# Moving a partition-group exchange from one load per group into four stores per pair, with one product stage a step later

## The chip, the core and the metric

The kernel runs on one NeuronCore of a Trainium2 chip, in one launch. The metric is device time in microseconds (us). Before the change, three runs took 1902.69, 1904.52 and 1907.6 us, so the median is 1904.52 us. Inputs and outputs are float32; each operand of a matmul is split into a high and a low part (float32r), and three products of the parts stand for one.

## The reference, cut to what matters

The input `x` has 2048 rows of 512. After a layer norm it goes through an attention with 32 heads over the last 512 cached keys and values, and through a gated branch, and the two are multiplied:

```python
xn = _layernorm(x)
# A: 32 heads, Dh = 128, keys and values cut to the last W = 512
q = (xn @ wq).reshape(B, Sq, Hq, Dh).transpose(0, 2, 1, 3)
scores = einsum("bhqd,bhkd->bhqk", q, k) * (Dh ** -0.5)
p = softmax(scores)
o = einsum("bhqk,bhkd->bhqd", p, v)
s = o.transpose(0, 2, 1, 3).reshape(B, Sq, Hq * Dh) @ wo
# B: z = gelu(xn @ w_in), halves z1 and layernorm(z2); w_sp mixes the rows
g = silu(((w_sp @ z2) + b_sp) * z1 @ w_out)
return x + s * g
```

The change concerns only how `p` is turned around between the softmax and the product with `v`, and when `q` is computed.

## The kernel before

The attention is cut into 128 blocks: one head and 512 query rows each (`NBLK = H * NQ`). A block has four steps of 128 query rows, and a counter `t` runs over all 512 steps, with a lead before and a tail after. The work is written as a software pipeline by hand: at each `t`, the loop at L680 to L730 issues one piece of each stage, and each stage works on a different block. The order in which a step's pieces are written is the order on each engine. For block b, whose first step is t = 4b:

- `score` (L468, steps 4b to 4b+3): three matmuls give a 128x512 tile of scores in PSUM, VectorE takes the negated maximum (L475), ScalarE the exponential with its row sums (L477). Rows of the tile are queries, columns are keys.
- `turn` (L479, one step later): the product with `v` needs keys on the partitions. VectorE transposes 32x32 squares (L486) into the tile `pB`, which holds two steps. This leaves four groups of 32 partitions that have yet to be exchanged among each other. The exchange goes through DRAM: after every second step one store (L491) writes `pB`, 128 rows of 4 KB, to `p_dram`.
- `turned` (L495, at t = 4b+7): four loads (L499) read the block back. Load a fills the 32 partitions 32a to 32a+31 of `pL`, with 8 pieces of 1 KB for each partition. These loads make the exchange.
- `shares` (L501, steps 4b+11 to 4b+14): ScalarE makes the high part `pT_h` (L506), GpSimd the low part `pT_l` (through the helper at L59).
- `pv` (L510, steps 4b+13 to 4b+16): three matmuls a step into a PSUM tile `ps_a`; `pv_out` (L515) at the last one makes `oT_h` and `oT_l`.
- `outp` (L526, steps 4b+18 to 4b+21): the product with `wo`, added to `sacc` by VectorE (L536).

`q` is computed in groups of four blocks (two heads, two query halves) in seven products instead of eight, `q_products` (L439), 42 matmuls spread over 16 steps, in three PSUM tiles `ps_a` of which one is held for the whole group. The group g starts at step 16g - `LEAD`, and everything that belongs to it is placed relative to that step: its weight loads (`load_q`, L405), the sums and splits of the weights on GpSimd and ScalarE, the evictions and the final `qT_h` and `qT_l` (`q_out`, L374; its VectorE part is put into the list `late` and issued at L728, at the end of the step). `ps_a` has four buffers (L83), shared by q's three tiles and by the tile of `pv`. The next tile to be allocated takes a buffer that is free, and its first matmul waits for the last reader of what stood there.

The other loads of this phase are pieces of 256 KB of weights, keys and values (`raw`, L102, and `wq`, L409), two a block, and, more rarely, parts of `x`. Every one of these transfers is issued by SyncE (SP), in program order. An issue that must wait for a semaphore holds up all issues behind it. After the attention follow the gated branch's products (L795 to L810) and the mixing of rows with the output (L951 to L977), which the change does not touch.

Of the kernel before, what the change touches and what calls it, by code (L numbers as in the profile page):

```python
# [8 lines left out]
F32 = mybir.dt.float32  # L9
# [8 lines left out]
P = 128  # L18
# [14 lines left out]

XL, QL, ML, PL, OL = 11, 7, 11, 13, 18
T8 = NT // 2
LEAD = 13
Q = 32


# [1 line left out]
def mixer_kernel(ctx: ExitStack, tc: tile.TileContext, x, wh, w_in, w_sp, b_sp, w_out, out):  # L41
# [8 lines left out]
    nc = tc.nc  # L50
# [3 lines left out]
    dram = ctx.enter_context(tc.tile_pool(name="dram", bufs=1, space=DRAM))  # L54
# [309 lines left out]
    pB = [None]  # L364
    qps, qT, pps, pD, pL, pT, oT, prob, sums = {}, {}, {}, {}, {}, {}, {}, {}, {}
# [23 lines left out]
    def qproj(b, c):  # L389
        h, qb = where(b)  # L390
        if c == 0:
            qps[b] = ps_acc.tile([P, 512], F32, name="ps_a")
        mm3(qps[b], c == 0, c == NC - 1, cols(wt[("q", h), 0], c * P, (c + 1) * P),
            tuple(X[0][c // 2, qb][:, a, c % 2] for a in range(2)))
# [84 lines left out]
    def turn(t):  # L479

        b, j = divmod(t, 4)
        if j % 2 == 0:
            pB[0] = ap.tile([P, 4, 2, P], F32, name="pB", bufs=3)
        nc.vector.transpose(pB[0][:, :, j % 2, :].rearrange("p a (c q) -> p a c q", q=Q),  # L486
                            prob.pop(t).rearrange("p (a c q) -> p a c q", a=4, q=Q))
        if j == 0:
            pD[b] = dram.tile([2, P, 1024], F32, name="p_dram", bufs=3)
        if j % 2:  # L490
            nc.sync.dma_start(pD[b][j // 2], pB[0].rearrange("p a j f -> p (a j f)"))  # L491
        if j == 3:
            nc.vector.reciprocal(sums[b], sums[b])

    def turned(b):  # L495
        pL[b] = ap.tile([P, 8, 256], F32, name="pL")
        of = pD.pop(b).rearrange("s (i r) (a f) -> a r (s i) f", i=4, a=4)
        for a in range(4):
            nc.sync.dma_start(pL[b][Q * a:Q * a + Q], of[a])  # L499

    def shares(b, c):  # L501
        hi = ap.tile([P, 512], F32R, name="pT_h", bufs=4)
# [68 lines left out]
    for g in range(1, NG):  # L571
        t0 = 16 * g - LEAD
        loads.setdefault(max(T0, t0 - 12), []).append(g)
# [20 lines left out]
    for k, d in enumerate((4, 6, 8, 11, 13, 15, 17)):  # L594
        for n in range(4):
            ends.setdefault(16 * (NG // 2 - 1) - LEAD + d + (0, 0, 1, 1)[n], []).append((fetch_part, 1, ORDER[k], n))
    ends.setdefault(16 * (NG - 1) - LEAD + 9, []).append((fetch_x, 1, (0, 1)))
    for k in ((0, 0), (1, 0)):
# [81 lines left out]
    for t in range(T0, T1):  # L680
# [9 lines left out]
        i = t + XL  # L690
# [12 lines left out]
        if 0 <= bq < 4:  # L703
            qproj(bq, cq)
        g, s = divmod(t + LEAD, 16)
        if 0 < g < NG:
# [15 lines left out]
        if 0 <= t - 1 < NSTEP:  # L722
            turn(t - 1)
        if t % 4 == 3 and 0 <= t // 4 - 1 < NBLK:
            turned(t // 4 - 1)
# [284 lines left out]
```

## Time and profile before

| what | value |
|---|---|
| three runs, median | 1904.52 us |
| the profiled execution, its own time | 1907.01 us |
| its span, from first to last instruction | 1905.1 us |
| granted TensorE clock, mean | 0.991 |
| steps of the attention, first store of p to last load | 55.4 to 1514.8 us |
| TensorE matmul busy in the span | 96% |
| mean busy share of the 16 DMA engines, 50 to 1510 us | 0.91 |

The page of the profile gives the busy time of each engine: PE is TensorE's matmuls, PEld its weight loads, DVE is VectorE, ACT ScalarE, POOL GpSimd, SP SyncE with the issues of transfers. A tile is named without its number; `pL<-p_dram` reads "into pL from p_dram". In a list of waits, "A <- B: 42.3, 30, 7.8" says that A's engine sat idle for 42.3 us in total, 30 times and at most 7.8 us at once, until B was done. In a table by stretches of time, the last columns are the granted clock, the mean busy share of the 16 DMA engines, and the GB/s that they moved. A share slightly over 1 comes from packets being counted whole in the stretch in which they begin.

### The profile page before, as it was taken

To read this page: it belongs to the slowest core of one execution; us is meant where nothing else is said; L and a number is where in the kernel's file an instruction comes from. 1 tells how busy PE (TensorE), PEld (TensorE's weight loads), DVE (VectorE), ACT (ScalarE), POOL (GpSimd) and SP (SyncE) were. 2 spreads that over 40 slices of the span, in tenths; PEclk is the share of its full clock that TensorE was granted. 3 is DMA by queue.
4 is the path that set the end of the run, shared out by engine and by line. 5 is a ranking of instruction groups with operands and counts; after the bars stand their busy time and mean duration, and the time that the engine had idled before them with its cause. 6 is when DMAs were issued, how large, how long until landed. Compare 5 with 4: busy or idle time off the path is not lost.

```text
span 1905.1 us, 28198 instructions
## 1 busy us (share of the span) xinstructions
PE 1820.5 (96%) x8658; PEld 1540.4 (81%) x8658; DVE 1403.3 (74%) x2497; ACT 1179.1 (62%) x2631; POOL 1244.3 (65%) x1185
## 2 busy tenths in 40 slices
PE   8898999999999898999999999999999999999999
PEld 7776777777787686778887877878777899999998
DVE  5687888888888787788888888888888556333433
ACT  4666677777677575667677777777677545333422
POOL 3686798798798786788878888888888435000000
PEclk9998999999999999999999999999999999999999
DMA  5798999999999889999889899988999833545543
GB/s 180 198 282 228 237 264 242 251 265 239 252 264 244 216 248 296 267 270 247 236 239 241 241 241 245 245 237 245 236 246 260 257 134 119 194 146 168 158 134 96
DMA packets 277624, 429.16 MB, mean 225 GB/s; under 512 B 22272, under 2 KB 183808, under 8 KB 276320
## 3 DMA queue, kind: packets, MB, share of 16 engines
q1 hardware_dynamic: 272864, 421.72, 79.4%
q10 hardware_dynamic: 4608, 5.64, 0.8%
q8 instruction: 68, 1.11, 0.3%
q14 instruction: 84, 0.69, 0.1%
HBM read 260.55 MB, written 166.72 MB: 224 GB/s over the span
## 4 chain that ended last, share of the span: by engine, by line
PE 73%; DMA 11%; DVE 7%; ACT 3%; POOL 3%; issue 2%; SPq 1%; ACTq 0%; POOLq 0%; DVEq 0%
PE ps_a L448 11%; PE ps L65 9%; PE ps L67 9%; PE ps L66 9%; PE ps_a L65 7%; PE ps_a L66 6%; PE ps_a L67 6%; DMA pL<-p_dram 4%; PE ps_g L66 4%; PE ps_g L67 4%; PE ps_g L65 4%; DMA p_dram<-pB 2%; DVE sacc L536 2%; DVE pB L486 1%; ACT prob L477 1%
## 5 line engine op out<-in xcount | busy, mean ns | idle before, releaser
L59 POOL TENSOR_TENSOR pT_l<-pL,pT_h 128x512 fp32r<-128x512 f32 x507 | 657.9, 1298 | 265.5 <-ACT pT_h L506 250.7
L477 ACT ACTIVATE prob<-ps,nm 128x512 f32<-128x512 f32 x512 | 352.8, 689 | 290.9 <-DVE nm L475 285.1
L536 DVE SCALAR_TENSOR_TENSOR sacc<-ps,sums,sacc 128x512 f32<-128x512 f32 x496 | 369.6, 746 | 149.2 <-PE ps L67 144.2
L506 ACT CAST pT_h<-pL 128x512 fp32r<-128x512 f32 x512 | 318.1, 621 | 130.8 <-DMA pL<-p_dram 68.3
L448 PE MATMUL ps_a<-x,x 128*128 128x512 f32 x1302 | 378.6, 391 | 7.9 <-ACT qs L455 6.9
L486 DVE STREAM_TRANSPOSE pB<-prob 128x512 f32<-128x512 f32 x512 | 359.0, 701 | 23.2 <-ACT prob L477 22.4
L475 DVE TENSOR_REDUCE nm<-ps 128x1 f32<-128x512 f32 x512 | 338.8, 662 | 8.6 <-PE ps L67 8.5
L448 PEld LDWEIGHTS ps_a<-x,x 128*128 128x128 f32 x1302 | 245.9, 189 | 61.9 <-ACT qs L455 8.3
L59 POOL TENSOR_TENSOR wl<-raw,wh 128x512 fp32r<-128x512 f32 x192 | 249.2, 1298 | 9.0 <-ACT wh L141 9.0
L65 PE MATMUL ps_a<-pT_h,wh 128*128 128x512 f32 x512 | 204.2, 399 | 46.7 <-DVE qT_l L728 42.3
L65 PE MATMUL ps<-wh,qT_h 128*128 128x512 f32 x512 | 204.0, 399 | 8.6 <-DVE sacc L536 5.1
L66 PE MATMUL ps_a<-pT_l,wh 128*128 128x512 f32 x512 | 203.0, 396 | 7.3 <-POOL pT_l L59 7.1
L67 PE MATMUL ps_a<-pT_h,wl 128*128 128x512 f32 x512 | 200.9, 392 | 0.0
L66 PE MATMUL ps<-wl,qT_h 128*128 128x512 f32 x512 | 200.9, 392 | 0.0
L65 PE MATMUL ps<-wh,oT_h 128*128 128x512 f32 x512 | 200.7, 392 | 0.0
L66 PE MATMUL ps<-wl,oT_h 128*128 128x512 f32 x512 | 200.6, 392 | 0.0
L67 PE MATMUL ps<-wh,oT_l 128*128 128x512 f32 x512 | 200.6, 392 | 0.0
L67 PE MATMUL ps<-wh,qT_l 128*128 128x512 f32 x512 | 200.6, 392 | 0.0
L66 PE MATMUL ps_g<-z_l,x 128*128 128x344 f32 x512 | 162.1, 317 | 1.3 <-POOL z_l L59 1.3
L65 PE MATMUL ps_g<-z_h,x 128*128 128x344 f32 x512 | 162.1, 317 | 0.0
L67 PE MATMUL ps_g<-z_h,x 128*128 128x344 f32 x512 | 161.9, 316 | 0.0
L65 PEld LDWEIGHTS ps_a<-pT_h,wh 128*128 128x128 f32 x512 | 96.7, 189 | 79.2 <-DVE qT_l L728 55.0
(203 smaller groups left out, 3235.3 us busy)
## 6 DMA issues: line engine op xcount, KB each, us to landing
p_dram<-pB SPq DMA_DIRECT2D x256, 512.0 KB, 5.2
pL<-p_dram SPq DMA_DIRECT2D x512, 256.0 KB, 5.8
raw<-wh SPq DMA_DIRECT2D x194, 256.0 KB, 6.7
wq<-wh SPq DMA_DIRECT2D x62, 256.0 KB, 6.1
x<-w_sp SPq DMA_DIRECT2D x60, 256.0 KB, 6.0
x_dram<-rawx SPq DMA_DIRECT2D x32, 256.0 KB, 5.6
x<-x_dram SPq DMA_DIRECT2D x28, 256.0 KB, 7.6
u_dram<-uB SPq DMA_DIRECT2D x15, 384.0 KB, 2.3
```

What stands on the lines that cost most here:

```text
L59: engine.tensor_tensor(lo, whole, hi.bitcast(F32), op=OP.subtract)
L65: nc.tensor.matmul(ps, lh, rh, start=first, stop=False)
L66: nc.tensor.matmul(ps, lh, rl, start=False, stop=False)
L67: nc.tensor.matmul(ps, ll, rh, start=False, stop=last)
L448: nc.tensor.matmul(qps[g, bank], wt["q", g, k][a][:, c * P:(c + 1) * P], X[g * 2 // H][ORDER[k]][:, b, c], start=first, stop=r == 5, skip_ ...
L475: nc.vector.tensor_reduce(nm, ps, axis=AX.X, op=OP.max, negate=True)
L477: nc.scalar.activation(prob[t], ps, AF.Exp, bias=nm, accum_out=sums[b][:, j:j + 1])
L486: nc.vector.transpose(pB[0][:, :, j % 2, :].rearrange("p a (c q) -> p a c q", q=Q), prob.pop(t).rearrange("p (a c q) -> p a c q", a=4, q=Q))
L506: nc.scalar.copy(h, p)
L536: nc.vector.scalar_tensor_tensor(at, ps, rs, at, op0=OP.mult, op1=OP.add)
```

## The change

The store of a pair becomes four stores. Store a takes columns 256a to 256a+255 of the pair's 1024 from all 128 partitions of `pB`, as 128 rows of 1 KB, and puts them where the group a of the exchanged tile belongs. `p_dram` of a block is now laid out as four groups a, 32 rows r, two pairs s, four pieces i and 256 elements. The load is a single one of 128 rows of 8 KB. In addition `LEAD` goes from 13 to 12, so every piece of q's work is issued one step later.

```diff
-LEAD = 13
+LEAD = 12
...
         if j == 0:
-            pD[b] = dram.tile([2, P, 1024], F32, name="p_dram", bufs=3)
+            pD[b] = dram.tile([4, Q, 2, 4, 256], F32, name="p_dram", bufs=3)
         if j % 2:
-            nc.sync.dma_start(pD[b][j // 2], pB[0].rearrange("p a j f -> p (a j f)"))
+            for a in range(4):
+                nc.sync.dma_start(pD[b][a, :, j // 2].rearrange("r i f -> i r f"),
+                                  pB[0].rearrange("p a j f -> p a (j f)")[:, a])
...
     def turned(b):
         pL[b] = ap.tile([P, 8, 256], F32, name="pL")
-        of = pD.pop(b).rearrange("s (i r) (a f) -> a r (s i) f", i=4, a=4)
-        for a in range(4):
-            nc.sync.dma_start(pL[b][Q * a:Q * a + Q], of[a])
+        nc.sync.dma_start(pL[b].rearrange("p k f -> p (k f)"), pD.pop(b).rearrange("a r s i f -> (a r) (s i f)"))
```

On the issuing engine SP, in the attention, this is a run of rows before the change. A row gives the line, the transfer and the sizes of the side that is written, outermost first; "x4" stands for four of the same in a row.

```order
L491 DMA p_dram<-pB 128x1024
L499 DMA pL<-p_dram 32x8x256 x4
L102 DMA raw<-wh 128x512
L491 DMA p_dram<-pB 128x1024 x2
L499 DMA pL<-p_dram 32x8x256 x4
L491 DMA p_dram<-pB 128x1024
L102 DMA raw<-wh 128x512 x2
```

The same run after it:

```order
L492 DMA p_dram<-pB 4x32x256 x4
L499 DMA pL<-p_dram 128x2048
L102 DMA raw<-wh 128x512
L492 DMA p_dram<-pB 4x32x256 x8
L499 DMA pL<-p_dram 128x2048
L492 DMA p_dram<-pB 4x32x256 x4
L102 DMA raw<-wh 128x512 x2
```

The places of stores and loads among the other issues stay, the counts change from two stores and four loads a block to eight stores and one load, and the side of a store in DRAM is now written as 4 times 32 rows of 256 elements, where the side in SBUF still has 128 rows.

On TensorE, at the second and third step of a group of q (where q's second tile `ps_a` begins, L448, next to the first matmul of a block's `pv`, L65), this stood before; the brackets name the engines whose semaphores a matmul waits for:

```order
L448 MATMUL ps_a<-x_180,x_737 128x512
L448 MATMUL ps_a<-x_181,x_737 128x512
L65 MATMUL ps_a<-pT_h,wh_6562 128x512 [waits DVE_49]
L66 MATMUL ps_a<-pT_l,wh_6562 128x512 [waits Pool_49]
L67 MATMUL ps_a<-pT_h,wl_6563 128x512
```

and this stands there now:

```order
L448 MATMUL ps_a<-x_180,x_757 128x512
L448 MATMUL ps_a<-x_181,x_757 128x512 [waits DVE_49,Activation_49]
L65 MATMUL ps_a<-pT_h,wh_8396 128x512
L66 MATMUL ps_a<-pT_l,wh_8396 128x512 [waits Pool_49]
L67 MATMUL ps_a<-pT_h,wl_8397 128x512
```

The `pv` matmul that took its buffer over from a `qT_l` of the step just before no longer has a wait for VectorE there; 30 such waits stood in the program, and none stands now. In its place q's second tile waits for an `oT_l` and an `oT_h` (ScalarE) that were issued more than a step earlier.

## The prediction

> **What bounds the kernel now.** I read the page first, for the busy engine, and the DMA part of it.
>
> ```profile
> span 1905.1 us, 28198 instructions
> PE 1820.5 (96%) x8658; PEld 1540.4 (81%) x8658; DVE 1403.3 (74%) x2497; ACT 1179.1 (62%) x2631; POOL 1244.3 (65%) x1185
> DMA packets 277624, 429.16 MB, mean 225 GB/s; under 512 B 22272, under 2 KB 183808, under 8 KB 276320
> p_dram<-pB SPq DMA_DIRECT2D x256, 512.0 KB, 5.2
> pL<-p_dram SPq DMA_DIRECT2D x512, 256.0 KB, 5.8
> wq<-wh SPq DMA_DIRECT2D x62, 256.0 KB, 6.1
> ...
> bsp<-b_sp SPq DMA_DIRECT2D x1, 8.0 KB, 9.3
> ```
>
> TensorE is busy for 96% of the span. The issue rows, of which three and the last stand here, count 1384 transfers in the DMA view. 16 times 1384 is 22144, and with the 128 rows of 64 B of `bsp` that makes the 22272 packets under 512 B. So each transfer of this kernel ended with 16 completion packets, one for each DMA engine: every one was dealt out to all 16.
>
> Next the stretch of the attention as a whole, in the table by stretches: PE busy, PEld, DVE, ACT, POOL, then clock, DMA share and GB/s.
>
> ```profile
> 50.00:1510.00 1460.00, 1387.58 (x6023) 1125.39 (x6022) 1201.98 (x2138) 1006.98 (x2346) 1178.65 (x1109) 0.99 0.91 248
> ```
>
> 1460 us for 128 blocks are 11.41 us a block. TensorE works 1387.58 / 128 = 10.84 us of it, and only 72.4 us are idle in the whole stretch. The DMA engines are busy for 0.91 of it: they are the second bound, close behind. The waits show what ends the idle time:
>
> ```profile
> ACT pT_h L506 <- DMA pL<-p_dram: 68.3, 26, 8.0
> PE ps_a L65 <- DVE qT_l L728: 42.3, 30, 7.8
> ```
>
> The block's load comes late 26 times, and 30 times the first `pv` matmul waits for the buffer that `qT_l` still reads.
>
> **What the transfers cost now.** Short stretches in which one kind of transfer flows give rates: the first microseconds and the later ones of a set of four loads, then keys and weights in rows of 2 KB, then stores of 4 KB rows.
>
> ```profile
> 1009.00:1009.50 0.50, 0.50 (x4) 0.41 (x3) 0.00 (x0) 0.50 (x3) 0.50 (x2) 1.00 0.94 311
> 1009.50:1012.50 3.00, 2.91 (x14) 2.10 (x12) 2.13 (x5) 2.34 (x7) 3.00 (x3) 1.00 1.06 215
> 1014.75:1016.25 1.50, 1.50 (x9) 1.22 (x8) 1.50 (x4) 0.73 (x2) 1.50 (x3) 1.00 0.89 337
> 1004.75:1006.75 2.00, 2.00 (x11) 1.65 (x10) 1.64 (x3) 0.91 (x2) 0.21 (x1) 1.00 0.94 371
> 1026.00:1027.50 1.50, 1.50 (x8) 1.27 (x7) 1.50 (x3) 1.50 (x4) 1.50 (x2) 1.00 0.88 355
> ```
>
> With the issues of SP beside them one sees which transfer is which (start, length, count):
>
> ```profile
> 1007.49 1.80 SPq L499 DMA_DIRECT2D pL<-p_dram  x4
> 1009.39 0.40 SPq L491 DMA_DIRECT2D p_dram<-pB  x1
> 1009.83 1.39 SPq L102 DMA_DIRECT2D raw<-wh  x2
> ```
>
> Divided by 16 engines: the loads' pieces of 1 KB begin at 311 / 16 = 19.4 GB/s an engine, 52.7 ns each, and fall to 215 / 16 = 13.4, 76.2 ns each. Rows of 2 KB go at 337 / 16 = 21.1, and stores of 4 KB rows at 371 / 16 = 23.2 GB/s. So the loads into 32 partitions run at 58% of the stores' rate. Speeding these up is what the change can gain.
>
> **The change part by part.**
>
> *The single load.* 1 MB a block in 128 rows of 8 KB, 8 rows and 65,536 B for each engine: at the stores' 23.2 GB/s 2.83 us, against 65,536 / 13.4 = 4.88 now. That is 2.05 us less of each engine's time a block, if it is dealt out to 16. Both its sides are written as 128 rows, like those of most transfers so far, and I take that.
>
> *The four stores.* Eight transfers a block, each of 128 pieces of 1 KB. Here the rows of the order matter: the DRAM side is now 4x32x256, the SBUF side still 128 rows. For work to be dealt out by rows, both sides have to be cut into the same number of shares along their outermost size. 128 and 128, or 32 and 32, can be cut in 16; 4 and 128 only in 4. No transfer of the trace has an outermost size that isn't a multiple of 16, so the trace does not show what happens; the bounds are 16 engines and 4. I take 4: an issue carries no more than the sizes and steps of both sides, and 4 is the largest count that both outermost sizes can be cut into. Then 12 of the 16 engines get none of these stores, and I take it that the same four get all of them: 8 x 128 / 4 = 256 pieces of 1 KB a block on each of the four.
>
> [...]
>
> *What a piece costs on such an engine.* The trace has no store in 1 KB pieces. Nearest are the first half microsecond of the 1 KB loads, 52.7 ns. The fast end is the stores' rate without its gaps, 355 / (16 x 0.88) = 25.2 GB/s, 40.6 ns. The slow end is that of the 1 KB loads under way, 76.2 ns. A cost below the fast end I exclude, since none of these stretches moves bytes faster on an engine. I take 52.7: same size, not yet held up.
>
> *The sum for one of the four engines, a block.* Stores 256 x 52.7 = 13.49 us. The load 2.83 us. Two pieces `raw` or `wq` of 256 KB, 32,768 B an engine, at 21.1 GB/s: 1.56 us. The rest is what the 248 GB/s over 11.41 us (2.83 MB) leave beside 2.10 MB of p and 0.52 MB of pieces: 0.21 MB, 13 KB an engine, 0.62 us. Together 18.5 us, where a block takes 11.41 now. This is a matter of throughput, not of delay: by program order the stores of two pairs (steps 4b+4 and 4b+6) are issued before the step that needs the previous load, so the four engines always have work queued, and the pace of the blocks is theirs. TensorE's 10.84 us, the other engines and SP fit in beside it.
>
> 128 x (18.5 - 11.41) = 907 us. The profiled execution took 1907.0 us (span 1905.1 and 1.9 around it), so 2814; it stood 2.5 over the median of the runs, so **2811 us**. The parts before and after the attention stay.
>
> *SP.* Per block, eight issues of stores and one load replace two and four. The durations:
>
> ```profile
> L491 SPq DMA_DIRECT2D p_dram<-pB x256: 319/327/1289, 55.4 to 1504.4; - x128
> L499 SPq DMA_DIRECT2D pL<-p_dram x512: 302/448/1700, 67.8 to 1514.8; - x171
> SPq L491 <- DVE pB L486: 530.7, 127, 14.9
> ```
>
> 9 x 0.33 = 3.0 us against 2 x 0.33 + 4 x 0.45 = 2.4: 0.6 us more a block, on a queue that sits in front of its stores for 530.7 us in all, 4.1 us a block, until VectorE has made `pB`. I cost it at nothing; without this cover it would be 0.6 x 128 = 77 us. The wait of the load for its pair's last store stays, and `raw` and `wq` are queued behind it, as now; they are issued six or more steps ahead, but with a late load they come late too, inside the same 18.5 us.
>
> *q one step later.* Its 31 groups lose the wait of 42.3 us above, as the order shows: the `pv` matmul has no wait for VectorE there now. The wait that q's second tile gets instead is for an `oT_l` issued over a step earlier, 11.41 / 4 = 2.9 us, and should be over. A `qT` is ready at the latest at the end of step 16g+2 for a first use at 16g+4, so a step of 2.9 us is left. Its weights `wq` are issued a step later as well, and still seven steps, 20 us, before the sums that read them, against 6.1 us to landing. In the forecast this gain is swallowed: TensorE waits for the load of p anyway. It is worth up to 42 us only where the stores do not bind.
>
> **The rivals.**
>
> *The stores go to 16 engines after all* (dealt out by pieces, or each of the four to other engines), and the kernel gets faster. For it: all 1384 transfers so far used 16. Against: none had a 4. An engine's time per block, now 0.91 x 11.41 = 10.4 us, would change by 64 x (52.7 - 44.2) ns = +0.5 for the stores (44.2 ns being 1 KB at 23.2 GB/s) and -2.05 for the load: 8.9 us, a share of 0.78. The late loads and the wait for `qT_l` go: 1907.0 - 42.3 - 2.5 = 1862 us, and not below 1907.0 - 72.4 - 2.5 = 1832, the idle time of the stretch. The point that decides is whether an engine's 18.5 us becomes less than TensorE's 10.84. [...]
>
> *Four engines, and they hold each other up.* The four walk 32 partitions each at the same pace, and may meet at the same part of SBUF, as the loads into 32 partitions do now, where 16 engines share a quarter of the partitions. At the slow end's 76.2 ns the stores alone take 19.5 us, the sum is 24.5, and 1907.0 + 128 x 13.1 - 2.5 = 3581 us. For it: the loads fall from 311 to 215 GB/s after half a microsecond and stay there. Against: only four engines read, not sixteen, and they need not stay in step.
>
> *Sixteen engines and no gain*, since the block's data is complete only when one large transfer is: 1905 us. A 1 MB load lands after 7.7 us, a quarter of it after 5.8:
>
> ```profile
> x<-x_dram SPq DMA_DIRECT2D x5, 1024.0 KB, 7.7
> ```
>
> That is 1.9 us later, but the fourth quarter is issued 3 x 0.45 = 1.3 us after the first, so it is nearly even.
>
> **How the numbers follow.** Forecast, four engines at or near 52.7 ns: 0.62. Four engines held up: 0.21. Sixteen and faster: 0.14. Sixteen and no gain: 0.03. With the fast end's rates an engine needs 10.4 + 2.6 + 1.4 + 0.5 = 14.9 us a block, 1907.0 + 128 x 3.5 - 2.5 = 2353 us. From there to the slow end's 3581 hold the first two cases, 0.83; the other two stay outside. Faster by over 0.3% (about what a measurement of this kernel can tell from no change) 0.14, within it 0.03, slower 0.83.
>
> **What would show it.** If four engines carry the stores, the packets under 512 B are 16 x (1384 - 768 + 128) + 4 x 1024 + 128 = 16128; if sixteen, 16 x 1768 + 128 = 28416. The mean DMA share falls while the kernel gets slower: four engines full and twelve busy for 5.0 of 18.5 us make 0.45, at 153 GB/s. ACT's wait for `pL<-p_dram` grows from 68.3 us to most of the 900 added, and stores land after 10 us or more instead of 5.2. TensorE then idles 7.7 us a block; should its granted clock fall for that, its work may stretch by as much at no cost. The wait of `ps_a L65` for `qT_l L728` is gone. The forecast is wrong if the small packets are 28416, or if the DMA share of the attention stays near 0.9.

## The result, and the profile after

The change makes the kernel slower: 2420.8 us in the median of four runs (2419.65 to 2421.35) against 1906.06 us for the kernel before, a ratio of 1.2697 with an interval of 1.2668 to 1.2727. The forecast was 2811 us, in a range of 2353 to 3581: the measured time lies 390 us below the forecast and 68 above the lower edge.

The page of the profile after, the lines that answer to those of before:

```profile
span 2419.1 us, 28699 instructions
PE 1995.5 (82%) x8658; PEld 1623.2 (67%) x8658; DVE 1424.0 (59%) x2497; ACT 1174.7 (49%) x2631; POOL 1238.9 (51%) x1185
DMA packets 255100, 429.17 MB, mean 177 GB/s; under 512 B 16128, under 2 KB 177664, under 8 KB 237408
DMA 42%; PE 29%; SPq 12%; ACT 5%; POOL 5%; issue 3%; DVE 3%; ACTq 0%; DVEq 0%; POOLq 0%
DMA p_dram<-pB 21%; DMA pL<-p_dram 16%; SPq L492 10%; PE ps_g L66 3%; PE ps_g L67 3%; PE ps_g L65 3%; POOL pT_l L59 3%; PE ps L65 3%; PE ps_a L448 2%; PE ps_a L66 2%; ACT prob L477 2%; PE ps_a L67 2%; PE ps_a L65 2%; PE ps L66 2%; PE ps L67 2%
```

The third line holds the count that the prediction named: 16128 packets under 512 B, which is 4 completions for each of the 1024 stores, 16 for each of the other 744 transfers, and the 128 rows of `bsp`. The last two lines are the chain of work that ended last. Before, the first of them read:

```profile
PE 73%; DMA 11%; DVE 7%; ACT 3%; POOL 3%; issue 2%; SPq 1%; ACTq 0%; POOLq 0%; DVEq 0%
```

TensorE made 73% of the chain before and makes 29% now; the stores, the load and the issue of stores on SP (SPq) make nearly half.

The stretch of the attention, in the table by stretches (PE, PEld, DVE, ACT, POOL, then clock, DMA share, GB/s), and 4 us in it in which only stores flow:

```profile
50.00:2020.00 1970.00, 1560.75 (x6024) 1206.36 (x6023) 1221.34 (x2137) 1003.07 (x2347) 1174.85 (x1113) 0.90 0.54 183
...
1221.00:1225.00 4.00, 3.60 (x15) 2.66 (x16) 2.59 (x6) 3.04 (x7) 4.00 (x4) 1.00 0.27 97
```

The stretch grew from 1460 to 1970 us, which is 510 of the 514 us that the profiled execution gained (2420.87 against 1907.01). Its mean DMA share fell from 0.91 to 0.54. The second row shows why a mean over 16 engines misleads here: stores alone, eight issued one behind the other, keep 0.27 of the engines busy, four of sixteen and a little. They move 97 GB/s, 24.2 for each of four engines, so a piece of 1 KB takes 42.2 ns. (The trace's record of such a packet lasts 46.0 ns on average there; on four engines the records must overlap a little, and that puts the share above 4/16.)

The queue of SP around that time (start, length, count), and the durations of the stores' issues:

```profile
1209.63 1.39 SPq L499 DMA_DIRECT2D pL<-p_dram  x1
1211.07 0.43 SPq L102 DMA_DIRECT2D raw<-wh  x1
1211.54 1.04 SPq L409 DMA_DIRECT2D wq<-wh  x2
1212.68 12.08 SPq L492 DMA_DIRECT2D p_dram<-pB  x8
1226.25 0.33 SPq L499 DMA_DIRECT2D pL<-p_dram  x1
```

```profile
L492 SPq DMA_DIRECT2D p_dram<-pB x1024: 502/1246/3980, 57.4 to 2018.7; - x171
```

Between two loads stand 16.6 us, about a block, and eight stores are issued in 12.1 of them. A store's issue has grown to a median of 1246 ns, from 327 for a store of four times the size. Whether this is the cause or an effect is what the experiments below must tell.

The waits, of ScalarE, VectorE and TensorE:

```profile
ACT pT_h L506 <- DMA pL<-p_dram: 606.1, 113, 10.9
...
PE ps L65 <- ACT prob L477: 194.5, 49, 11.4
...
DVE pB L486 <- DMA p_dram<-pB: 143.0, 117, 4.7
...
PE ps_a L65 <- ACT pT_h L506: 95.1, 52, 7.0
...
PE ps_a L448 <- DVE oT_l L59: 20.2, 22, 1.6
```

ScalarE now waits 113 times for the load of one of the 128 blocks, 606.1 us in all against 68.3, and VectorE waits 143 us until stores have left a buffer of `pB` free, against 0.7. The `pv` matmul's wait for `qT_l` is gone from the list. q's second tile waits 20.2 us for `oT_l` in its place.

### The profile page after: what moved, and what is told of

Same layout as the page of the kernel before. It is cut to its first block, busy times and chain, and to the rows that moved or that the text cites. A ratio compares the mean times of both kernels' runs of the same rounds, so it can differ in the third digit from the quotient of the medians.

```text
span 2419.1 us, 28699 instructions
## 1 busy us (share of the span) xinstructions
PE 1995.5 (82%) x8658; PEld 1623.2 (67%) x8658; DVE 1424.0 (59%) x2497; ACT 1174.7 (49%) x2631; POOL 1238.9 (51%) x1185
## 2 busy tenths in 40 slices
DMA packets 255100, 429.17 MB, mean 177 GB/s; under 512 B 16128, under 2 KB 177664, under 8 KB 237408
## 4 chain that ended last, share of the span: by engine, by line
DMA 42%; PE 29%; SPq 12%; ACT 5%; POOL 5%; issue 3%; DVE 3%; ACTq 0%; DVEq 0%; POOLq 0%
DMA p_dram<-pB 21%; DMA pL<-p_dram 16%; SPq L492 10%; PE ps_g L66 3%; PE ps_g L67 3%; PE ps_g L65 3%; POOL pT_l L59 3%; PE ps L65 3%; PE ps_a L448 2%; PE ps_a L66 2%; ACT prob L477 2%; PE ps_a L67 2%; PE ps_a L65 2%; PE ps L66 2%; PE ps L67 2%
## 5 line engine op out<-in xcount | busy, mean ns | idle before, releaser
L506 ACT CAST pT_h<-pL 128x512 fp32r<-128x512 f32 x512 | 316.7, 619 | 636.7 <-DMA pL<-p_dram 606.1
L448 PE MATMUL ps_a<-x,x 128*128 128x512 f32 x1302 | 406.9, 412 | 35.3 <-DVE oT_l L59 20.2
L65 PE MATMUL ps<-wh,qT_h 128*128 128x512 f32 x512 | 227.5, 444 | 187.9 <-ACT prob L477 180.4
L448 PEld LDWEIGHTS ps_a<-x,x 128*128 128x128 f32 x1302 | 261.4, 201 | 103.5 <-ACT pT_h L506 29.4
L65 PE MATMUL ps_a<-pT_h,wh 128*128 128x512 f32 x512 | 220.4, 431 | 95.1 <-ACT pT_h L506 95.1
L66 PE MATMUL ps_a<-pT_l,wh 128*128 128x512 f32 x512 | 226.0, 441 | 56.8 <-POOL pT_l L59 56.6
L65 PEld LDWEIGHTS ps<-wh,qT_h 128*128 128x128 f32 x512 | 106.1, 207 | 239.3 <-ACT prob L477 199.7
L65 PE MATMUL ps<-wh,oT_h 128*128 128x512 f32 x512 | 213.4, 417 | 26.5 <-ACT prob L477 14.1
L66 PE MATMUL ps<-wl,qT_h 128*128 128x512 f32 x512 | 215.6, 421 | 0.0
L67 PE MATMUL ps<-wh,qT_l 128*128 128x512 f32 x512 | 214.0, 418 | 0.4 <-DVE qT_l L59 0.4
L65 PEld LDWEIGHTS ps_a<-pT_h,wh 128*128 128x128 f32 x512 | 104.6, 204 | 137.9 <-ACT pT_h L506 117.8
L59 DVE TENSOR_TENSOR oT_l<-ps_a,oT_h 128x256 fp32r<-128x256 f32 x256 | 96.3, 418 | 163.9 <-ACT oT_h L521 163.9
L66 PEld LDWEIGHTS ps_a<-pT_l,wh 128*128 128x128 f32 x512 | 104.9, 205 | 109.7 <-POOL pT_l L59 90.3
```

What stands on the lines that cost most here:

```text
L59: engine.tensor_tensor(lo, whole, hi.bitcast(F32), op=OP.subtract)
L65: nc.tensor.matmul(ps, lh, rh, start=first, stop=False)
L66: nc.tensor.matmul(ps, lh, rl, start=False, stop=False)
L67: nc.tensor.matmul(ps, ll, rh, start=False, stop=last)
L448: nc.tensor.matmul(qps[g, bank], wt["q", g, k][a][:, c * P:(c + 1) * P], X[g * 2 // H][ORDER[k]][:, b, c], start=first, stop=r == 5, skip_ ...
L506: nc.scalar.copy(h, p)
```

## The experiments

**Theory A:** the outermost count of 4 on the DRAM side puts every store on the same four DMA engines, and their throughput sets the pace. **Theory B:** eight issues a block instead of two, or writing in pieces of 1 KB, cost the time, whichever engines carry them. Ratios are to the kernel before, run on the same chip, with their intervals.

| run | written side of a store | LEAD | median us | ratio | packets under 512 B |
|---|---|---|---|---|---|
| after | 4x32x256 | 12 | 2420.8 | 1.2697 (1.2668 to 1.2727) | 16128 |
| exchange alone | 4x32x256 | 13 | 2433.2 | 1.2779 (1.2741 to 1.2816) | 16128 |
| two engines | 2x32x256 | 12 | 3809.58 | one run | 16128 |
| eight engines, exchange left out | 8x16x256 | 12 | 1872.71 | 0.9820 (0.9788 to 0.9851) | 20224 |
| 128 rows, exchange left out | 128x256 | 12 | 1839.66 | 0.9643 (0.9625 to 0.9661) | 28416 |
| by 32 partitions | 32x4x256 | 12 | 1850.96 | 0.9704 (0.9682 to 0.9726) | 28416 |
| by 32 partitions | 32x4x256 | 13 | 1887.64 | 0.9916 (0.9893 to 0.9939) | 28416 |
| by 32 partitions, order 0, 2, 1, 3 | 32x4x256 | 12 | 1848.7 | 0.9709 (0.9689 to 0.9729) | 28416 |
| LEAD alone, exchange in the loads | 128x1024 | 12 | 1854.18 | 0.9721 (0.9702 to 0.9741) | 22272 |
| the same, loads in the order 0, 2, 1, 3 | 128x1024 | 12 | 1848.21 | 0.9702 (0.9682 to 0.9723) | 22272 |

**Other engines, same pieces.** The stores of a pair are cut by the 32 source partitions instead of by the target columns:

```diff
-            for a in range(4):
-                nc.sync.dma_start(pD[b][a, :, j // 2].rearrange("r i f -> i r f"),
-                                  pB[0].rearrange("p a j f -> p a (j f)")[:, a])
+            for i in range(4):
+                nc.sync.dma_start(pD[b][:, :, j // 2, i].rearrange("a r f -> r a f"),
+                                  pB[0].rearrange("p a j f -> p a (j f)")[Q * i:Q * i + Q])
```

> The kernel after, with each pair's four stores cut by the 32 source partitions instead of by the 256 target columns: same number of stores, same pieces of 1 KB, same places in DRAM, same single load, same LEAD of 12; the written side is now 32x4x256 instead of 4x32x256. Theory A (the outermost count of 4 puts all stores on four DMA engines): 16 completions for each store, so 28416 packets under 512 B, the DMA share near 0.9, and 1860 to 1910 us. Theory B (eight issues a block, or writing in pieces of 1 KB, cost the time, on whichever engines): stays at 2350 to 2450 us.

1850.96 us, 9 us under the span that A gave, and faster than before; the DMA share is 0.84, where A had it near 0.9. Number of stores, bytes, size of a piece and places in DRAM are those of the change. What differs is which pieces go together in a store (32 partitions with all four groups, not 128 partitions with one) and with it the outermost count that is written. Its stretch and its issues:

```profile
50.00:1462.00 1412.00, 1382.44 (x6080) 1134.62 (x6079) 1210.16 (x2148) 1009.50 (x2358) 1184.49 (x1115) 0.99 0.84 257
```

```profile
L492 SPq DMA_DIRECT2D p_dram<-pB x1024: 302/433/1995, 57.4 to 1454.1; - x171
```

TensorE is idle for only 29.6 us of 1412. The issue of a store of the same size takes 433 ns here, not 1246. So B as it was stated falls, and the long issues after the change come with the four engines; that an issue is held up while these engines work off the stores before it is the likely reading, and the two-engine run below bears it out.

**Sixteen engines and all partitions.** `p_dram` is laid out by source partition, so both sides of a store have 128 rows.

```diff
-            pD[b] = dram.tile([4, Q, 2, 4, 256], F32, name="p_dram", bufs=3)
+            pD[b] = dram.tile([4, P, 2, 256], F32, name="p_dram", bufs=3)
...
-                nc.sync.dma_start(pD[b][a, :, j // 2].rearrange("r i f -> i r f"),
+                nc.sync.dma_start(pD[b][a, :, j // 2],
...
-        nc.sync.dma_start(pL[b].rearrange("p k f -> p (k f)"), pD.pop(b).rearrange("a r s i f -> (a r) (s i f)"))
+        nc.sync.dma_start(pL[b].rearrange("p k f -> p (k f)"), pD.pop(b).rearrange("a (q w) s f -> (a q) (w s f)", w=4))
```

> The kernel after with p_dram laid out by the 128 source partitions: the four stores of a pair are 128 rows of 1 KB on both sides, the load is 128 rows of 8 KB of the same bytes. The exchange of the groups is thereby left out, and p's elements meet the wrong rows of v. Theory A: all 16 engines and all of SBUF for both, 64 x 42.6 ns = 2.7 us of stores and 2.8 us of load an engine and block, a DMA share near 0.7, no late loads, no wait for qT_l: 1835 to 1870 us. Theory B: stays at 2350 to 2450 us.

1839.66 us, as A said. This is the rival of sixteen engines, measured; the four engines cost 2420.8 - 1839.7 = 581 us against it. The DMA share was a miss:

```profile
50.00:1450.00 1400.00, 1378.30 (x6068) 1132.44 (x6067) 1208.92 (x2147) 1008.05 (x2356) 1183.78 (x1114) 0.99 0.82 260
```

0.82, not 0.7. The same bytes at the rates of undisturbed stretches make less. The packets of this trace show where it lies: the load's rows of 8 KB took 393 ns on average against a median of 309, rows of 2 KB 121 against 84, and the stores' pieces 47.0 against 46. That transfers slow each other down where they mix is the likely reading; it was not tested.

**Two engines.** Each store is cut in two of 64 partitions, so that the written side is 2x32x256:

```diff
             for a in range(4):
-                nc.sync.dma_start(pD[b][a, :, j // 2].rearrange("r i f -> i r f"),
-                                  pB[0].rearrange("p a j f -> p a (j f)")[:, a])
+                for i in (0, 2):
+                    nc.sync.dma_start(pD[b][a, :, j // 2, i:i + 2].rearrange("r i f -> i r f"),
+                                      pB[0].rearrange("p a j f -> p a (j f)")[Q * i:Q * i + 2 * Q, a])
```

> The kernel after, with each store cut into two of 64 partitions, so that the written side is 2x32x256: 16 stores a block of 64 KB, the same bytes and the same pieces of 1 KB. Theory A: each store runs on two engines, the same two each time, so an engine has 512 pieces a block. With what the profile after shows, 47 pieces in 0.5 us on four engines or 42.6 ns a piece, and 4.5 us for the rest, 21.8 + 4.5 = 26.3 us a block against 15.4: 2421 + 128 x 10.9 = 3816 us, and 16128 packets under 512 B (2 for each store). Theory A without a fixed pair of engines: under 2450 us. Theory B (cost per issue on SP, 1.25 us each in the profile after): 16 issues of 1.25 us are 20 us a block, 2421 + 128 x 4.6 = 3010 us; if an issue of half the size takes half the time, unchanged at 2421.

3809.58 us, where A gave 3816. The stretch of the attention and the issues:

```profile
50.00:3420.00 3370.00, 1972.35 (x6105) 1463.38 (x6104) 1223.23 (x2150) 1007.72 (x2359) 1172.84 (x1115) 0.75 0.32 108
```

```profile
L493 SPq DMA_DIRECT2D p_dram<-pB x2048: 477/1276/3835, 57.2 to 3409.9; - x187
```

3370 / 128 = 26.3 us a block, as worked out ahead from the four engines' numbers. The DMA share is 0.32. 16128 small packets are 2 for each of 2048 stores. The two engines must be the same for every store: had the pairs been spread, the 16 would have shared the work.

Slow issues on SP are the rival to look at here. The 16 issues of a block at 1.28 us are 20.4 us, with the load and the other pieces SP issues for 24.5 of the 26.3 us in the trace, and the chain that ended last gives SP nearly half:

```profile
SPq 49%; DMA 24%; PE 12%; ACT 5%; issue 4%; DVE 3%; POOL 2%; ACTq 0%; POOLq 0%; DVEq 0%
```

But an issue does not need that long: the first four stores of the attention, with none before them, and the 16 of two later pairs:

```profile
57.23 2.25 SPq L493 DMA_DIRECT2D p_dram<-pB  x4
92.19 23.01 SPq L493 DMA_DIRECT2D p_dram<-pB  x16
```

The first four take 0.56 us each, the later ones 1.44. In the profile after, where the median is 1.25 us, a quarter of the issues took 0.54 us or less, and 11 of the 12 stores that SP issued after 1.5 us or more without an issue took 0.50 to 0.66. So an issue by itself needs about half a microsecond here, and the rest of its time it is held up. In the two-engine run the median distance from one store's issue to the next is 1.32 us, which is 32 pieces of 41 ns on each of two engines: the issues go at the engines' pace. A run with the same issues shared out over two issuing engines was not made.

**Eight engines.** `p_dram` is padded so that the written side is 8x16x256.

```diff
-            pD[b] = dram.tile([4, Q, 2, 4, 256], F32, name="p_dram", bufs=3)
+            pD[b] = dram.tile([4, 8, 8704], F32, name="p_dram", bufs=3)
...
-                nc.sync.dma_start(pD[b][a, :, j // 2].rearrange("r i f -> i r f"),
+                nc.sync.dma_start(pD[b][a, :, :8192].rearrange("u (v s f) -> u v s f", v=16, s=2)[:, :, j // 2],
...
-        nc.sync.dma_start(pL[b].rearrange("p k f -> p (k f)"), pD.pop(b).rearrange("a r s i f -> (a r) (s i f)"))
+        nc.sync.dma_start(pL[b].rearrange("p k f -> p (k f)"), pD.pop(b)[:, :, :8192].rearrange("a u (w x) -> (a u) w x", w=4))
```

> The kernel after with p_dram padded so that the written side of a store is 8x16x256: same eight stores a block of 128 pieces of 1 KB, single load in rows of 8 KB, LEAD 12. The exchange of the groups is left out, as in the run with stores of 128 rows, so p's elements meet the wrong rows of v. Theory A (the outermost count sets the number of engines): 8 completions a store, 16 x 744 + 8 x 1024 + 128 = 20224 packets under 512 B; an engine has 128 x 42.3 ns = 5.4 us of stores and 4.5 us of the rest, 9.9 us a block, under TensorE's 10.8, so 1838 to 1860 us and no sign of the four engines' 2421. Rival (any store whose two sides are written with different outermost counts runs on four engines, or is slow in itself): 2300 us or more, and 16128 packets.

The packets are 20224, exactly 8 a store, and the time is 1872.71 us: most of the loss is gone, but it is 13 us over the span expected and 33 us over the run with 128 rows. The stretch and the load's wait:

```profile
50.00:1490.00 1440.00, 1392.17 (x6088) 1137.92 (x6087) 1210.66 (x2149) 1010.66 (x2358) 1184.17 (x1114) 0.99 0.77 254
```

```profile
ACT pT_h L506 <- DMA pL<-p_dram: 69.5, 42, 6.9
```

A mean share of 0.77 hides that these eight engines, by the sum above, would need 9.9 us of a block of 11.25. Loads still come late 42 times. That so little slack lets small delays through is a reading; it was not tested.

**The two parts apart.** First the exchange alone, with `LEAD` at 13:

> The kernel after with LEAD back at 13: the exchange in the stores alone. If the four engines' 15.4 us a block set the pace, q's step is hidden behind them: 2410 to 2430 us, as with LEAD 12. If q's step adds to the exchange: 2470 us, the 53 us that the step alone gave (1907 to 1854) on top.

2433.2 us, close over the first span: q's step is worth about 12 us here, 0.5%, not nothing (a ratio of 1.2779 against 1.2697, and the intervals do not meet). In this run the `pv` matmul waits for `qT_l` more than the 42.3 us of before; why was not taken apart. The wait and the stretch:

```profile
PE ps_a L65 <- DVE qT_l L728: 160.5, 30, 9.5
...
50.00:2030.00 1980.00, 1542.24 (x6007) 1222.64 (x6006) 1217.85 (x2135) 1002.10 (x2345) 1171.38 (x1110) 0.87 0.54 182
```

TensorE is idle for 437.8 us of the stretch here and for 409.3 with the step moved (1970 - 1560.75), so all but 28.5 of the 160.5 us come back as other waits. Then the step alone:

> The kernel before with LEAD 12 instead of 13, nothing else: q's work one step later, stores and loads of p as before. If the wait of the pv matmul for qT_l (42.3 us in the profile before) is time that nothing else would take: 1862 us or a little more, a ratio near 0.98. If TensorE would lose the same time to late loads of p: 1890 to 1905 us, a ratio of 0.99 to 1.0. In both cases the row PE ps_a L65 <- DVE qT_l L728 is gone.

1854.18 us, 53 us less than before on the same chip, and more than either answer gave. The row is gone, and the stretch looks like this:

```profile
50.00:1460.00 1410.00, 1378.21 (x6041) 1129.31 (x6041) 1204.92 (x2140) 1007.02 (x2352) 1182.21 (x1113) 0.99 0.92 257
```

TensorE now is idle for 31.8 us of 1410, at a DMA share of 0.92. ScalarE's wait for the load falls from 68.3 to 27.6 us, with the loads unchanged, so the late loads of before were hardly a bound of their own. And the stores by 32 partitions without the step:

> The stores cut by 32 source partitions, on 16 engines, with LEAD 13. If the gain of the run with LEAD 12 (1851 us) is q's step and the exchange in the stores is worth some 3 us by itself: 1885 to 1905 us. If the stores' cut by itself removes late loads, and with them most of what q's step gave: 1850 to 1870 us.

1887.64 us, in the first span: a gain of 17.5 us by itself, where with the step it adds 3 (1850.96 against 1854.18, inside the intervals). The gains overlap, and the step is the larger. The wait it removes is still there in this run:

```profile
PE ps_a L65 <- DVE qT_l L728: 36.2, 30, 4.8
```

**Does the order of partition groups matter?** Two runs with one line changed each, `(0, 2, 1, 3)` in place of `range(4)`, first in the stores by 32 partitions:

> The stores cut by 32 source partitions with LEAD 12, issued in the order of partition groups 0, 2, 1, 3 instead of 0, 1, 2, 3. If 1 KB pieces take 53.5 ns instead of 46 there because transfers one behind the other read the same half of SBUF's partitions (0 to 63, then 64 to 127), alternating halves shortens them: nearer 47 ns, 1842 to 1850 us. If 32 partitions hold up a transfer whatever stands before and after it: 53 ns and 1851 us.

Then in the loads of the kernel before, with `LEAD` 12:

> The exchange in the loads as before, LEAD 12, the four loads issued in the order of partition groups 0, 2, 1, 3. If successive loads into the same half of the partitions hold each other up, the 76 ns of a piece fall to 50 to 60 and the time from 1854 to 1842 to 1850 us; if each load of 16 pieces an engine is long enough to be held up by itself: 70 ns or more and 1850 to 1855 us.

The mean time of a 1 KB packet in the traces went from 53.5 to 52.6 ns in the stores, and from 76.0 to 72.1 in the loads: by the packets the second answer in both. The times decide nothing: 1848.7 and 1848.21 us lie in the spans of the first answers, but do not differ from the runs without the new order by more than the intervals.

Four versions with `LEAD` 12 that keep the exchange beat both kernels, with ratios from 0.9702 to 0.9721. The runs do not tell them apart.

## Why the prediction was right, and where a size was off

- **The four engines** were the step on which all hung, and they were right. I took the four from the outermost sizes of the two sides, and the same four for every store, as an estimate; the profile before showed neither. The runs do: an outermost count of 4 or 2 on the written side gave 4 or 2 completions a store (16128 packets under 512 B in both), a count of 8 gave 8 (20224), and counts of 32 and 128 gave 16 (28416). The times with `LEAD` 12 go with it: 3809.58 us with 2, 2420.8 with 4, 1872.71 with 8, 1850.96 with 32 and 1839.66 with 128. The runs also agree that with a count of 2 or 4 the set is a fixed one, since the two-engine kernel loses 1389 us to the four-engine one. Which engines they are, no run shows.
- **The size that was off is the cost of a piece.** I took 52.7 ns, from 1 KB loads into 32 partitions in their first half microsecond. Measured were 42.2, close to the fast end of 40.6, from the stores' own rate without gaps. So the row to take was the one of the same direction, though of another size. 256 x 10.5 ns are 2.7 of the 3.1 us by which the block came out shorter (15.4 instead of 18.5). The remaining terms, by subtraction, came to 15.4 - 10.8 = 4.6 us instead of 5.0. The 0.62 stood for a cost at or near 52.7 ns; the time fell near where the fast end puts it, so the mechanism was right and the central figure was not.
- **Throughput, not delay**: the sum of one engine's work gave the pace of the blocks within its terms, and with the piece and the rest as measured on four engines it gave the two-engine kernel within 0.2%. The engines that wait are VectorE for `pB` and ScalarE for `pL`, as forecast. ScalarE's wait for the load grew by 538 us, about what the kernel lost.
- **TensorE**: its busy time in the stretch grew from 1387.6 to 1560.8 us at a granted clock of 0.90. That is 12.2 us a block, which fits into 15.4, as the prediction allowed. With two engines it is 1972 us at 0.75, 15.4 a block of 26.3.
- **SP** I costed at nothing, at 0.33 us an issue. An issue took 1.25 us, but 0.43 with 16 engines, and about 0.5 with four where none stood before it: most of its growth came with the bound.
- **q's step** I called worth up to 42 us where the stores don't bind, and swallowed where they do. It gave 53 us alone and about 12 beside the four engines. In the profiled executions TensorE's idle time fell by 40.5 us (84.6 to 44.1), as sized, and its busy time by 12.0 us (1820.5 to 1808.5), which the prediction had not counted. The largest part of these 12 us, 3.5, is in the first matmul of `pv`, which took 399 ns on average before and 392 then; the rest is spread over others. The row of the weight loads of the same matmuls comes near the sum of both; whether it is the better row in general, or is near by chance, no run shows:

```profile
PEld ps_a L65 <- DVE qT_l L728: 55.0, 30, 8.3
```

- **Where a gain could come from**: the prediction saw it in faster loads. The exchange in the stores on 16 engines gave 17.5 us by itself and 3 beside q's step, which is inside the intervals; q's step alone gave 53. The rival of sixteen engines had the time about right, but most of its gain is the step's.
- **The rival of engines that hold each other up** (3581 us) did not come: a piece took 42.2 ns where stores flow alone, and the record of a 1 KB packet lasts 46.2 ns on average in the whole stretch, about as much as the 46.0 there. The rival of sixteen engines was sized at 1862 with a floor of 1832; its kernel measured 1839.7. The rival without gain is met by none of the runs on 16 engines with `LEAD` 12, though the exchange added little to what the step gave.
- **The DMA share** I gave as 0.45 at 153 GB/s; 0.54 at 183 came out. 2.83 MB over 15.4 us make 184 GB/s, so the rate follows from the block's time. The share does not: 10.8 us on four engines and 4.6 on all make 0.47. The packet records give 11.8 and 5.4 us, which make the 0.54; their sum of 17.2 us is more than the block of 15.4, so on the four engines records overlap. The page of the profile gives no landing times for these stores, so that sign stayed unread.

## What to carry to other kernels

Before a transfer is rewritten, look at the outermost size of both its sides as the program carries them: in these runs a store whose written side had an outermost count of 2, 4 or 8 went to as many DMA engines, and one with 32 or 128 to all 16, with 2 and 4 always the same ones, and with these two the mean DMA share fell to 0.32 and 0.54, from 0.91, while the kernel starved. The count of packets under 512 B, with those of the other transfers taken off and divided by the number of the stores, shows it at once: (16128 - 16 x 744 - 128) / 1024 = 4 after the change. When an exchange between partitions must be cut into pieces somewhere, cut it so that 32 or 128 rows stand outermost on both sides (1850.96 us with 32 and, the exchange left out, 1839.66 with 128, against 2420.8 with 4); and when two changes come together, run each alone, since here the smaller-looking one, a step's shift in the order, held nearly the whole gain and the other hid it.

## What the runs showed of the hardware that was not expected

- A store that reads 32 partitions in 1 KB pieces is slowed much less than a load that writes 32 partitions: 53.5 ns a packet on average (stores by 32 partitions, `LEAD` 12) against 76.0 (`LEAD` alone), where stores from 128 partitions take 47.0 (128 rows).
- The time of SP's issue grows when few engines serve the transfers: a median of 433 ns with 16 engines, 575 with 8, 1246 with 4, and 1276 with 2 for half the size. With 4 and 2 most of it is being held up, since the shortest issues there took 502 and 477 ns; with 8 it is not, since the shortest took 568.
